# The projection into u in seven quarter products, and one explicit list of steps, in a block attention with a gated MLP

## The chip, the cores and the metric

The kernel runs on one core of one Trainium2 chip. The metric is the time of one execution on the device in microseconds (us), the median of several runs. A profiled execution gives the trace; its span is counted from the first to the last instruction. The engines are PE (TensorE, matmuls; PEld is its weight load), DVE (VectorE), ACT (ScalarE), POOL (GpSimd) and SP (SyncE, which issues the transfers here). SPq is the queue of SP.

## The reference

Attention within chunks of 64 tokens, for 8 batches, 8 heads, 576 tokens and head size 64; its output x, as a matrix of 576 x 512 for each batch, goes through a gated MLP.

```python
scores = scale * np.matmul(q_c, k_c.transpose(0, 1, 2, 4, 3))     # chunks of 64
attn = softmax(scores)                                            # over the chunk
x = np.matmul(attn, v_c)                                          # per batch 576 x 512
h = gelu_tanh(x @ w_in)                                           # w_in 512 x 1024
u, v = h[..., :512], h[..., 512:]
v_n = (v - mean(v)) / np.sqrt(var(v) + 1e-06) * g_ln
v_s = np.einsum('ts,bsd->btd', w_sg, v_n) + b_sg[None, :, None]   # w_sg 576 x 576
out = x + (u * v_s) @ w_out                                       # w_out 512 x 512
```

## The kernel before

The 36 attention tiles of 128 tokens (four and a half make a batch of 576 tokens) and the MLP of 8 batches run as one stream. A matrix product in full accuracy is made of three matmuls on fp32r operands: every operand is held as a high part and a low part (`xh`, `xl` for x; `gh`, `gl` for the gated product; `win_h`, `win_l` for w_in), and low x high, high x low and high x high are added up in PSUM.

The steps of a tile t: `att_load` (SP loads q, k and v), `att_scores` (S for one tile, P for a pair; matmuls into the two `banks` of PSUM, then the softmax on DVE, ACT and POOL), `att_transpose` (T; from tile 5 on the 32x32 blocks are transposed on DVE, copied by ACT, and four quarters of 32 partitions are swapped: `ptT<-blocks`, two copies on ACT, two on DVE by `SWAP_ON_ACT`) and `att_out` (O, or Q for a pair; matmuls into a `pm` buffer of PSUM, then the split into `xh`, `xl` and the plain `xf` in `keep`).

The steps of a batch b: `v_unit` (v0 to v3, and in each even batch v4 for the odd rows of two batches: 12 matmuls of 512 columns, gelu on ACT, statistics on DVE, the power -1/2 on POOL in line 545, then scaling and splitting), `u_unit` (u0 to u3: 24 matmuls of 128x288, line 573, and a gelu into the tile `u2`), `s_unit` (s0 to s3: the product of w_sg with v, 28 matmuls, then the multiplication with u on DVE) and the product with w_out. That last one is written in seven products of quarters for batches from `QUARTERS_FROM` = 2 on (Strassen's scheme in Winograd's form): `o_product` p1, p5, p2, p6, p3, p7, p4, each 12 matmuls of 128x288 in line 660. Sums of w_out's quarters are made once by POOL (`sum_step`) and kept in the DRAM tensor `factors`; `load_factor` brings each product's factor back into a ring of four places. Batches 0 and 1 use `o_unit` with whole w_out.

`pm` has three buffers in PSUM. The tile `u2` has one buffer: it holds u of a batch, then the gated product and its sums, then three of four quarters of the output until the stores to `out_dram` have read them.

w_in and w_out come as float64; `pair_begin` and `pair_end`, and `double_begin` and `double_end`, make high and low parts from their words on ACT, DVE and PE (lines 136 to 189). `START` lists the steps of the weights and of batches 0 and 1 (W and w: a quarter of w_in's v half; X and x: of its u half; Y: an eighth of w_out; B, C and K: the factors). From batch 2 on, the last loop of the function writes v's, u's, s's and p's in a fixed order and puts the attention of later tiles behind units by `SLOTS`. A step writes all its instructions at once. The framework's scheduler then orders the instructions of each engine by its own costs; only the matmuls of batches from 2 on (`pin`) and a few others keep the program's order. Each engine works through its own order strictly.

Of the kernel before, what the change touches and what calls it, by code (L numbers as in the profile page):

```python
# [17 lines left out]
ALU = mybir.AluOpType  # L18
# [27 lines left out]
START = """  # L46
L0 A0 S0 D8 L1 L2 A1 L3 S1 W0 w0 W1 w1 A4 S2 T0 O0 T1 O1 W2 T2 w2 X0 M0 W3 w3 S3 O2
S4 T3 O3 v00 x0 X1 X2 T4 v01 v02 O4 x1 x2 X3 v03 G0 A8 u00 g0 P5 g1 x3 g2 g3 u01 v04 g4 T5
u02 T6 u03 s00 P7 Q5 s01 s02 T7 T8 s03 v10 Y0 Q7 Y1 v11 Y2 u10 u11 Y3 v12 Y4 v13 u12 Y5 Y6 Y7 A10
u13 o00 P9 s10 T9 T10 s11 s12 A12 A14 s13 P11 Q9 o01 B0 o02 B1 B2 T11 B3 o03 T12 A15 o10 B4 C5 o11 B5  # L50
B6 S13 T13 Q11 o12 B7 C6 o13 B8 B9 A17 v20 v21 C7 O13 K0 P14 v22
"""

PE_TILES = 5

SWAP_ON_ACT = (1,)
# [4 lines left out]

SLOTS = {
    1: "v1:T0 v1:T1 u0:S23 u0:T2 u0:O01 s0:T3 s0:S4 s0:O23 s3:T4 p6:S56",
    0: "v0:O4 u0:T5 u2:S78 s0:T6 s1:O56 s2:T8 p5:T7 p3:S9A p3:O78",
}

QUARTERS_FROM = 2
PRODUCTS = (1, 5, 2, 6, 3, 7, 4)  # L70
RING = 4
# [4 lines left out]
SINGLE_ON_ACT = False  # L76
# [14 lines left out]
def block_attention_gated_mlp(ctx: ExitStack, tc: tile.TileContext, qkv, w_in, w_out, w_sg, g_ln, b_sg, out):  # L91
# [10 lines left out]
    def split(hi, lo, src, hi_eng, lo_eng):  # L102
        if hi_eng is nc.scalar:
            nc.scalar.copy(hi, src)  # L104
        else:
            hi_eng.tensor_copy(hi, src)
        lo_eng.tensor_tensor(lo, src, hi.bitcast(F32), op=ALU.subtract)  # L107


# [22 lines left out]

    def pick(step):
        return nc.gpsimd if step in ON_POOL else nc.vector

    def high_word(f, hw):

        nc.scalar.activation(f.bitcast(F32), hw.bitcast(F32), AF.Abs, scale=2.0**16)  # L140
        nc.vector.tensor_scalar(f.bitcast(F32), f.bitcast(F32), ZERO64, TOP64, op0=ALU.max, op1=ALU.min)
        nc.vector.tensor_scalar(f, f, 4, 1, op0=ALU.logical_shift_left, op1=ALU.logical_shift_right)
        nc.vector.scalar_tensor_tensor(f, hw, -0x80000000, f, op0=ALU.bitwise_and, op1=ALU.bitwise_or)

    def double_begin(n, st, eng):

        raw, fi, ri = st[:, : 2 * n], st[:, 2 * n : 3 * n], st[:, 3 * n : 4 * n]
# [15 lines left out]

    def pair_begin(n, st):
# [6 lines left out]
        high_word(f, pair[:, :, 1])  # L171
# [3 lines left out]
        q, lw, top = words[:, :n], words[:, 1::4], p.bitcast(U16)[:, 1::2]  # L175
        nc.vector.scalar_tensor_tensor(q, lw, 9, top, op0=ALU.logical_shift_right, op1=ALU.bitwise_or)

    def pair_end(n, hi, lo, st):
# [3 lines left out]
        ps = ps_m.tile([P, 2, 512], F32, name="pm")[:, 0, :n]  # L182
        shape = lambda a: a.rearrange("p (k c) -> p k c", k=hi.shape[1]) if len(hi.shape) == 3 else a
        nc.scalar.mul(hi, shape(f), -1.0)
        terms = [(ident, f), (low[0], q), (low[1], p), (ident_r, hi)]
        for i, (a, c) in enumerate(terms):
            out_ps = shape(ps) if c is hi else ps
            nc.tensor.matmul(out_ps, a, c, start=(i == 0), stop=(i == len(terms) - 1))  # L188
        nc.scalar.mul(lo, shape(ps), -1.0)
# [28 lines left out]
    def u_w_begin(dt):  # L218
        pair_begin(DH, staged["u", dt])

    def u_w_end(dt):
        cols = slice(dt * P, (dt + 1) * P)
        pair_end(DH, win_h[:, :, cols], win_l[:, :, cols], staged["u", dt])

    def o_w(et, half):
# [8 lines left out]
        double_begin(n, st, pick("Z"))  # L234
        double_end(n, wout_h[:, rows, cols], wout_l[:, rows, cols], st, pick("Y"))


    factors = nc.dram_tensor("factors", (7, P, 2, 2, 2 * P), F32).ap()
    ring, loads, sums = [], [0], []
# [4 lines left out]
    def load_factor():  # L244
        n = loads[0]
        loads[0] += 1
        if n < 7 * (B - QUARTERS_FROM):
            nc.sync.dma_start(out=factor_place(n).bitcast(F32), in_=factors[n % 7])

    def quarters():  # L250
        return [
            a[:, 2 * c : 2 * c + 2, 2 * r * P : 2 * (r + 1) * P] for r in range(2) for c in range(2) for a in (wout_h, wout_l)
        ]

    def sum_step(n):
# [12 lines left out]
        tc.keep_in_program_order(nc.gpsimd.tensor_tensor(o, a, c, op=op))  # L268

    def keep_factor(p, parts):  # L270
        for a, part in enumerate(parts):
            tc.keep_in_program_order(nc.sync.dma_start(out=factors[PRODUCTS.index(p), :, a], in_=part.bitcast(F32)))

    def split_sum(p):

        hi, lo = (
            tmp.tile([P, S], F32R, name="fac", tag="tmp")[:, : 4 * P].rearrange("p (k e) -> p k e", k=2) for _ in range(2)
        )
        src = sums[(5, 6, 7, 3).index(p)]
        tc.keep_in_program_order(nc.scalar.copy(hi, src))  # L280
        nc.vector.tensor_tensor(lo, src, hi.bitcast(F32), op=ALU.subtract)
        keep_factor(p, (hi, lo))
        if p == 3:
            for i in range(2):
                r = const.tile([P, KT * DM], F32R, name=f"ring_{i}", tag=f"wout_{i}")
                ring.append(r.rearrange("p (n a k e) -> p n a k e", n=2, a=2, k=2))
            for _ in range(RING):
                load_factor()

    def keep_quarters(_):  # L290
        parts = quarters()
        for p, i in ((1, 0), (2, 2), (4, 6)):
            keep_factor(p, parts[i : i + 2])
# [14 lines left out]
    def split_w_sg(i):  # L308
        nonlocal wsg_h, wsg_l
        st, odd, bt = staged["s"]  # L310
        if i == 0:
            wsg_h, wsg_l = (w_sg_tile(i).rearrange("p (i s) -> p i s", i=5) for i in range(2))
            nc.gpsimd.memset(wsg_l[64:128, 4, :].bitcast(F32), 0.0)
        hi, lo = wsg_h[:, i, :], wsg_l[:, i, :]
        if i < 4:
            split(hi, lo, st[:, i, :], nc.scalar, nc.vector)
            return
        nc.scalar.copy(hi, odd)
        nc.vector.tensor_tensor(lo[0:ODD], odd[0:ODD], hi[0:ODD].bitcast(F32), op=ALU.subtract)
# [60 lines left out]
    pinned = [False]  # L380

    def pin(ins):
        if pinned[0]:
            tc.keep_in_program_order(ins)

    def att_scores(*tiles):

        if tiles[0] < PE_TILES:
            for t in tiles:
# [6 lines left out]
                softmax((t,), sc)  # L396
            return
        for i, t in enumerate(tiles):
            qt = state[t]
            sc = banks[:, :, i * HP * D : (i + 1) * HP * D].rearrange("p c (hp s) -> p c hp s", hp=HP)  # L400
            for h in range(H):
                for c in range(2):
                    r, o = slice(c * D, (c + 1) * D), half(t, h, c)
                    pin(nc.tensor.matmul(sc[o, c, h // 2, :], qt[r, 0, h, :], qt[r, 1, h, :], start=True, stop=True))  # L404
# [428 lines left out]
```

## Time and profile before

| | us |
|---|---|
| median of 3 runs | 500.79 (500.75 to 500.91) |
| the profiled execution | 500.32 |
| its span | 498.5 |
| mean granted PE clock in it | 1.00 |

The page gives for each engine the time in which it was busy, as a share of the span; matmuls overlap, so a busy PE isn't PE at its peak rate. The chain that ended last is followed back from the last instruction, at each step to what released it. A row of a group has the line, engine, operation, output and inputs with their shapes and count, then the busy time, the mean of one in ns, and the idle time ahead of it with what ended it. The rows that the prediction rests on are shown there.

### The profile page before, as it was taken

How to read it: one execution, taken by the hardware profiler on the slowest of the kernel's cores; microseconds unless marked ns; L12 is line 12 of the kernel's file. 1: busy time of each engine (PE TensorE's matmuls, PEld its weight loads, DVE VectorE, ACT ScalarE, POOL GpSimd, SP SyncE). 2: the span in 40 equal slices, each digit the busy share in tenths (PEclk: the TensorE clock that was granted, in tenths of full speed). 3: DMA queues.
4: the chain of work that ended last, by engine and by line, in shares of the span. 5: the costliest groups of instructions: out<-in, count | busy, mean ns of one | idle time of the engine just before them, and what ended most of it. 6: DMA issues, size and time to landing. Idle time of an engine off the chain costs nothing.

```text
span 498.5 us, 12331 instructions
## 1 busy us (share of the span) xinstructions
PE 485.9 (97%) x5167; PEld 449.6 (90%) x5172; DVE 378.1 (76%) x697; ACT 281.5 (56%) x489; POOL 89.1 (18%) x82
## 2 busy tenths in 40 slices
PE   5989999999999999999999999999999999999996
PEld 4667899899999899989999899988999899998996
DVE  7898769987789875988589675998679675876065
ACT  5798777753445775566752574557752564543130
POOL 0113000121084222022210312022120322002000
PEclk9999999999999999999999999999999999999999
DMA  8858001256146971694348600695447700181006
GB/s 330 304 170 241 6 3 43 87 152 169 56 145 220 275 257 52 208 264 169 87 126 258 197 1 11 202 283 162 120 128 228 226 1 1 48 291 55 0 10 212
DMA packets 61355, 72.27 MB, mean 145 GB/s; under 512 B 36082, under 2 KB 47858, under 8 KB 61300
## 3 DMA queue, kind: packets, MB, share of 16 engines
q1 hardware_dynamic: 61300, 71.49, 46.6%
q8 instruction: 40, 0.66, 0.5%
q14 instruction: 15, 0.12, 0.1%
HBM read 58.36 MB, written 13.11 MB: 143 GB/s over the span
## 4 chain that ended last, share of the span: by engine, by line
PE 88%; DVE 7%; ACT 2%; DMA 2%; SPq 0%; issue 0%; POOL 0%; ACTq 0%
PE pm L593 22%; PE pm L573 21%; PE pm L536 19%; PE pm L660 14%; PE pm L713 5%; PE banks L404 3%; PE pm L492 3%; DMA qkv_t<-qkv 2%; PE pm L188 1%; ACT pt L425 1%; DVE pt L433 1%; DVE nmax L417 1%; DVE gl L107 1%; DVE gt L602 1%; DVE xl L107 0%; PE banks L473 0%
## 5 line engine op out<-in xcount | busy, mean ns | idle before, releaser
L593 PE MATMUL pm<-wsg,v 128*128 128x288 f32 x768 | 108.1, 296 | 0.0
L593 PEld LDWEIGHTS pm<-wsg,v 128*128 128x128 f32 x768 | 103.8, 189 | 0.5
L545 POOL TENSOR_TENSOR sm<-sm,neg_half 128x1 f32<-128x1 f32 x36 | 36.9, 1024 | 152.0 <-DVE sm L544 139.8
L433 POOL TENSOR_TENSOR pt<-pt,den 128x1024 f32<-128x1024 f32 (+1 forms) x15 | 26.0, 1733 | 171.2 <-DVE den L431 157.3
L573 PE MATMUL pm<-xl,win_h 128*128 128x288 f32 x256 | 55.3, 297 | 1.0 <-DVE xl L107 1.0
L573 PE MATMUL pm<-xh,win_l 128*128 128x288 f32 x256 | 55.5, 298 | 0.0
L573 PE MATMUL pm<-xh,win_h 128*128 128x288 f32 x256 | 55.0, 296 | 0.0
L536 PE MATMUL pm<-win_h,xl 128*128 128x512 f32 x128 | 51.2, 400 | 0.2 <-ACT pt L425 0.2
L536 PE MATMUL pm<-win_h,xh 128*128 128x512 f32 x128 | 50.7, 396 | 0.0
L536 PE MATMUL pm<-win_l,xh 128*128 128x512 f32 x128 | 50.6, 395 | 0.0
L553 ACT ACTIVATE v<-hs,sm 128x512 fp32r<-128x512 f32 x32 | 23.2, 724 | 43.4 <-POOL sm L545 43.3
L104 ACT CAST gh<-u 128x576 fp32r<-128x576 f32 x24 | 16.2, 675 | 48.5 <-POOL u L617 29.7
L573 PEld LDWEIGHTS pm<-xh,win_l 128*128 128x128 f32 x256 | 41.5, 188 | 1.3
L573 PEld LDWEIGHTS pm<-xl,win_h 128*128 128x128 f32 x256 | 41.1, 188 | 1.3 <-DVE xl L107 1.3
L573 PEld LDWEIGHTS pm<-xh,win_h 128*128 128x128 f32 x256 | 41.0, 188 | 0.0
L660 PE MATMUL pm<-gh,ring 128*128 128x288 f32 x192 | 40.3, 296 | 0.0
L554 DVE SCALAR_TENSOR_TENSOR v<-hs,sm,v 128x512 fp32r<-128x512 f32 x32 | 24.0, 750 | 18.5 <-ACT v L553 18.3
L598 DVE TENSOR_TENSOR u<-pm,u 128x576 f32<-128x576 f32 x24 | 18.1, 753 | 20.4 <-PE pm L593 20.3
L660 PE MATMUL pm<-tv,ring 128*128 128x288 f32 x216 | 32.2, 297 | 0.0
L542 DVE BATCH_NORM_STATS2 sm<-hs 128x6 f32<-128x512 f32 x36 | 24.5, 683 | 9.9 <-ACT hs L539 9.8
L660 PEld LDWEIGHTS pm<-gh,ring 128*128 128x128 f32 x192 | 31.4, 188 | 0.1
L428 ACT ACTIVATE pt<-pt 128x1024 f32<-128x1024 f32 (+1 forms) x19 | 18.0, 949 | 22.2 <-DVE pt L427 21.9
(146 smaller groups left out, 1018.8 us busy)
## 6 DMA issues: line engine op xcount, KB each, us to landing
ring<-factors SPq DMA_DIRECT2D x42, 512.0 KB, 4.6
qkv_t<-qkv SPq DMA_DIRECT2D x32, 512.0 KB, 4.7
qkv_t<-qkv SPq DMA_DIRECT2D x124, 64.0 KB, 3.9
out_dram<-u SPq DMA_DIRECT2D x18, 288.0 KB, 5.2
out_dram<-ot SPq DMA_DIRECT2D x14, 288.0 KB, 2.7
qkv_t<-qkv SPq DMA_DIRECT2D x3, 768.0 KB, 7.6
wsg<-w_in SPq DMA_DIRECT2D x4, 512.0 KB, 5.3
wout<-w_in SPq DMA_DIRECT2D x4, 512.0 KB, 7.0
```

Of the source, the lines that this page charges most:

```text
L428: nc.scalar.activation(pt, pt, AF.Exp, scale=scale)
L433: eng.tensor_tensor(pt, pt, den.unsqueeze(2).broadcast_to([P, n, D]), op=ALU.mult)
L536: pin(nc.tensor.matmul(pv, a[:, kt, tok], c[:, kt, DH:], start=(i == 0), stop=(i == 11)))
L542: nc.vector.bn_stats(st, h)
L545: nc.gpsimd.tensor_tensor(rs, rs, neg_half, op=ALU.pow)
L553: nc.scalar.mul(hi, h, rs)
L554: nc.vector.scalar_tensor_tensor(lo, h, rs, hi.bitcast(F32), op0=ALU.mult, op1=ALU.subtract)
L573: pin(nc.tensor.matmul(pm[:, j, :HS], a[:, kt, dc], c[:, kt, j * HS : (j + 1) * HS], start=(i == 0), stop=(i == 11)))
L593: pin(nc.tensor.matmul(pm[:, j, :HS], a[:, dc], c[:, m, j * HS : (j + 1) * HS], start=(i == 0), stop=(i == len(ops) - 1)))
L598: nc.vector.tensor_tensor(g, pm[:, :, :HS], g, op=ALU.mult)
L660: pin(nc.tensor.matmul(pm[:, e, :HS], a[:, k, e * P : (e + 1) * P], c[:, k, :], start=starts and i == 0, stop=i == len(ops) - 1, skip_grou ...
L713: nc.tensor.matmul(pm[:, j, :HS], a[:, kt, ec], c[:, kt, j * HS : (j + 1) * HS], start=(i == 0), stop=(i == len(ops) - 1),)
```

## The change

1. From batch 2 on the projection into u is made of seven products of quarters as well. `u_product` (q1, q5, q2, q6, q3, q7, q4) has 12 matmuls each and collects in three `pm` buffers; x and z of them are added up as in `o_product`, and the gelu follows each finished quarter. Three results are copied out of PSUM by ACT, three are added by DVE.
2. The right factors of q5, q7, q6 and q4 are sums of x's quarters. `x_quarters` (z25, z27, z26, z24 for batch 2) makes them: a sum on POOL into the quarter (1, 0) of `u2`, a cast on ACT into the high part, a subtraction on DVE for the low part, in the tile `xt`, which takes over the place of w_in's u half.
3. The left factors are sums of w_in's quarters, made once: `sum_product` (E0 to E3) adds high and low parts by matmuls with the identity and with its negative, and ACT and DVE split the result. They go to `factors`, which has 14 rows now, and the ring loads 84 factors in place of 42.
4. w_in's two halves are tiles of their own (`wv_h`, `wv_l`; `wu_h`, `wu_l`).
5. `SWAP_ON_ACT` is (0, 1): all four swaps of a tile's transposition are on ACT. `SINGLE_ON_ACT` is True: the softmax of the single tiles 13, 22 and 31 is made by eight exponentials on ACT with their sums.
6. Every step is a generator that stops (`yield`) before each instruction that another engine must have prepared. `ORDER` lists the whole program as some 2,400 entries; each entry runs one step on to its next stop. `tc.manual_schedule()` keeps every engine's instructions in that order. The loads of the ring (`f`) and of tiles (`A`) are entries too.

```diff
+SWAP_ON_ACT = (0, 1)
+ORDER = """
+L0 L1 A0 M0 L2 L3 A1 W0 A2 A3 W0 A4 W1 W0 W0 W1 w0 W0 W1 S0 W0 W1 w0 w1 S0 W2 W1 S0 W1 S0
...
+v30 p27 p23 f16 P18 p27 P18 P18 p24 v30 v30 Q16 v30 f17 p24 v30 T19 p24 v31 Q16 v31 A20 T18 T19 Q16 v30 T19 T19 v30
...
-SINGLE_ON_ACT = False
+SINGLE_ON_ACT = True
...
+    ctx.enter_context(tc.manual_schedule())
...
+    wu = wu_tile("wu").rearrange("p (a k c) -> p a k c", a=2, k=KT)
+    wu_h, wu_l = wu[:, 0], wu[:, 1]
...
-    factors = nc.dram_tensor("factors", (7, P, 2, 2, 2 * P), F32).ap()
+    factors = nc.dram_tensor("factors", (14, P, 2, 2, 2 * P), F32).ap()
+    order = [i for b in range(O_QUARTERS_FROM, B) for i in ([*range(7)] if b >= U_QUARTERS_FROM else []) + [*range(7, 14)]]
...
+    def sum_product(n):
...
+        pos, neg = (((h21, l21, h22, l22), ()), ((), (h11, l11)), ((), (h12, l12)), ((h11, l11), (h21, l21)))[n]
+        terms = [(ident_r, a) for a in pos] + [(held["neg"], a) for a in neg]
+        for i, (a, c) in enumerate(terms):
+            nc.tensor.matmul(
+                ps, a, c, start=n in (0, 3) and i == 0, stop=i == len(terms) - 1, skip_group_check=n in (1, 2)
+            )
+        yield
+        hi, lo = factor_tiles()
+        nc.scalar.mul(hi, ps, -1.0 if n == 2 else 1.0)
...
+    def x_quarters(b, p):
...
+        begin_u(b)
+        t = quarter_of(u2[b], 1, 0)
+        a, c = {5: (x(0, 1), x(0, 0)), 7: (x(1, 1), x(0, 1)), 6: (t, x(0, 0)), 4: (x(1, 0), t)}[p]
+        X_SUM[p].tensor_tensor(t, a, c, op=ALU.add if p == 6 else ALU.subtract)
+        hi, lo = x_right[p]
+        yield
+        nc.scalar.copy(hi, t)
+        yield
+        X_LOW[p].tensor_tensor(lo, t, hi.bitcast(F32), op=ALU.subtract)
+
+    def u_product(b, p):
+        at = {1: "x", 5: "y", 2: "z", 6: "x", 3: "y", 7: "x", 4: "x"}[p]
+        starts = p in (1, 5, 2)
...
+        ops = [(a, c, k) for k in range(2) for a, c in ((wl, hi), (wh, lo), (wh, hi))]
+        for e in range(2):
+            for i, (a, c, k) in enumerate(ops):
+                nc.tensor.matmul(
+                    pm[:, e, :HS], a[:, k, e * P : (e + 1) * P], c[:, k, :],
+                    start=starts and i == 0, stop=i == len(ops) - 1, skip_group_check=not starts,
+                )
+        yield
...
+        if p in (1, 5, 6):
+            nc.scalar.copy(o, src) if p in U_KEPT_ON_ACT else nc.vector.tensor_copy(o, src)
+            return
+        if p != 4:
+            nc.vector.tensor_tensor(o, src, o, op=ALU.add)
+            yield
+        nc.scalar.activation(o, src if p == 4 else o, AF.Gelu_apprx_tanh, scale=-1.0)
...
+    begun = {}
+    for step in ORDER.split():
+        if step not in begun:
+            begun[step] = iter(steps[step[0]](int(step[1:])) or ())
+        next(begun[step], None)
```

POOL's order in the part of batch 3 in which its v's and u's are made (`sm` is the statistics of a v, `pt` a softmax, the number behind u is that of the tile `u2` of a batch). Before:

```order
30 L433 TENSOR_TENSOR pt<-pt,den 128x1024
31 L545 TENSOR_TENSOR sm<-sm,neg_half 128x1 x4
32 L433 TENSOR_TENSOR pt<-pt,den 128x1024
33 L617 TENSOR_TENSOR u_3016<-u_3016 128x288
34 L433 TENSOR_TENSOR pt<-pt,den 128x512
```

and now:

```order
34 L667 TENSOR_TENSOR sm<-sm,neg_half 128x1
35 L763 TENSOR_TENSOR u_3011<-xf 128x2x288
36 L667 TENSOR_TENSOR sm<-sm,neg_half 128x1
37 L763 TENSOR_TENSOR u_3011<-xf 128x2x288
38 L667 TENSOR_TENSOR sm<-sm,neg_half 128x1
39 L763 TENSOR_TENSOR u_3011<-u_3011,xf 128x2x288
40 L667 TENSOR_TENSOR sm<-sm,neg_half 128x1
41 L763 TENSOR_TENSOR u_3011<-xf,u_3011 128x2x288
42 L539 TENSOR_TENSOR pt<-pt,den 128x1024
```

The four sums of x's quarters (L763) stand between the powers of the four v's, and the first of them is the first to write batch 3's `u2`.

SP's order at the end of batch 2: the ring's loads, the stores of the output's quarters (p2 from `ot`, the other three from `u2`) and the loads of the next attention tiles. Before:

```order
72 L671 DMA out_dram<-u_2337 128x2x288
73 L372 DMA qkv_t<-qkv 128x1024
74 L377 DMA qkv_t<-qkv 64x4x64 x4
75 L372 DMA qkv_t<-qkv 128x1024
76 L377 DMA qkv_t<-qkv 64x4x64 x4
77 L248 DMA ring_2306<-factors 128x1024
78 L671 DMA out_dram<-u_2337 128x2x288
79 L248 DMA ring_2307<-factors 128x1024
80 L671 DMA out_dram<-u_2337 128x2x288
```

and now:

```order
75 L860 DMA out_dram<-ot 128x2x288
76 L311 DMA ring_2171<-factors 128x1024 x2
77 L860 DMA out_dram<-u_2245 128x2x288
78 L311 DMA ring_2170<-factors 128x1024
79 L860 DMA out_dram<-u_2245 128x2x288
80 L311 DMA ring_2170<-factors 128x1024
81 L860 DMA out_dram<-u_2245 128x2x288
82 L476 DMA qkv_t<-qkv 128x1024
83 L481 DMA qkv_t<-qkv 64x4x64 x4
```

The last two stores stood behind the loads of two attention tiles; now all stand ahead of them.

ACT's order in the start, up to the cast of tile 1's x (`xh<-xf`, its second), which the first v waits for (`wsg_`, `wout_` are the places in which w_in's quarters are staged). Before:

```order
19 L189 ACTIVATE win_l<-pm 128x512
20 L104 CAST xh<-xf 128x2x4x64
21 L445 COPY ptT<-banks 128x512
22 L522 CAST xodd_285<-xh 128x4x64
23 L522 CAST xodd_286<-xl 128x4x64
24 L140 ACTIVATE wsg_201<-wsg_201 128x512
25 L184 ACTIVATE win_h<-wout_159 128x512
26 L512 COPY xf<-banks 128x2x4x64
27 L189 ACTIVATE win_l<-pm 128x512
28 L104 CAST xh<-xf 128x2x4x64
```

and now:

```order
20 L186 ACTIVATE wsg_188<-wsg_188 128x512
21 L526 ACTIVATE pt,den<-pm,nmax 128x64 x8
22 L552 COPY ptT<-banks 128x512
23 L531 ACTIVATE pt<-pt 128x512
24 L186 ACTIVATE wsg_215<-wsg_215 128x512
25 L186 ACTIVATE wout_256<-wout_256 128x512
26 L248 ACTIVATE wv_l<-pm 128x512
27 L552 COPY ptT<-banks 128x512
28 L240 ACTIVATE wu<-wsg_188 128x4x128
29 L622 COPY xf<-banks 128x2x4x64
30 L640 CAST xodd_324<-xh 128x4x64
31 L624 CAST xh<-xf 128x2x4x64
```

Passes for the first three quarters of w_in's u half (188, 215, 256) have moved ahead of that cast, and 188 ahead of tile 2's exponentials (row 21).

More of the change, by code (lines that the diff above doesn't have):

```diff
@@ L40 @@
 QKV_BUFS = 4
[L46 to L51, printed above, removed]
-"""
-PE_TILES = 5
-SWAP_ON_ACT = (1,)
@@ L267, in sum_step, with keep_factor @@
         )[n]
[L268 to L270 removed]
+        nc.gpsimd.tensor_tensor(o, a, c, op=op)
+    def keep_factor(of, p, parts):
+        row = PRODUCTS.index(p) + (7 if of == "o" else 0)
         for a, part in enumerate(parts):
[L272 removed]
+            nc.sync.dma_start(out=factors[row, :, a], in_=part.bitcast(F32))
@@ L281, in split_sum @@
         nc.vector.tensor_tensor(lo, src, hi.bitcast(F32), op=ALU.subtract)
[L282 to L291, printed above, removed]
+        yield
+        keep_factor("o", p, (hi, lo))
@@ L292, in keep_quarters, with begin_ring @@
+    def begin_ring():
+        for i in range(2):
+            r = const.tile([P, KT * DM], F32R, name=f"ring_{i}", tag=f"wout_{i}")
+            ring.append(r.rearrange("p (n a k e) -> p n a k e", n=2, a=2, k=2))
+        for _ in range(RING):
+            load_factor()
+    def keep_quarters(of):
+        parts = quarters(of)
         for p, i in ((1, 0), (2, 2), (4, 6)):
-            keep_factor(p, parts[i : i + 2])
+            keep_factor(of, p, parts[i : i + 2])
     def load_w_sg():
@@ L403, in att_scores @@
                     r, o = slice(c * D, (c + 1) * D), half(t, h, c)
-                    pin(nc.tensor.matmul(sc[o, c, h // 2, :], qt[r, 0, h, :], qt[r, 1, h, :], start=True, stop=True))
-        softmax(tiles, banks[:, :, : len(tiles) * HP * D].rearrange("p c (k s) -> p c k s", s=D))
+                    nc.tensor.matmul(sc[o, c, h // 2, :], qt[r, 0, h, :], qt[r, 1, h, :], start=True, stop=True)
+        yield from softmax(tiles, banks[:, :, : len(tiles) * HP * D].rearrange("p c (k s) -> p c k s", s=D))
     def softmax(tiles, sc):
@@ L564, in block_attention_gated_mlp, with begin_u @@
     u2 = {}
+    def begin_u(b):
+        if b not in u2:
+            u2[b] = mp.tile([P, KT, S], F32, name="u2", tag="u2")
     def u_unit(b, dt):
@@ L684, in o_product @@
             add(ot, held[1])
-            store(0, 0, ot)
+            yield from store(0, 0, ot)
         elif p == 6:
@@ L690, in o_product @@
             add(o, o)
-            store(0, 1, o)
+            yield from store(0, 1, o)
         elif p == 7:
@@ L700, in o_product @@
             add(o, o if last else x(1, 0))
-            store(1, 0, o)
+            yield from store(1, 0, o)
     def o_unit(b, et):
```

444 lines of the change are left out of this document (276 added, 168 removed).

## The prediction

> **What bounds the kernel now.** I read the head of the page first, then the chain that ended last in order of time, then the waits of TensorE.
>
> ```profile
> span 498.5 us, 12331 instructions
> PE 485.9 (97%) x5167; PEld 449.6 (90%) x5172; DVE 378.1 (76%) x697; ACT 281.5 (56%) x489; POOL 89.1 (18%) x82
> PE 88%; DVE 7%; ACT 2%; DMA 2%; SPq 0%; issue 0%; POOL 0%; ACTq 0%
> ...
> PE pm L395 <- DMA qkv_t<-qkv: 6.1, 2, 5.8
> PE pm L573 <- DVE xl L107: 1.0, 1, 1.0
> ```
>
> TensorE (PE) is busy for 97% of the span and the chain runs through it for 88%. Its only waits are the first load and one microsecond on DVE. Busy time alone proves little, because matmuls overlap, so the chain in order of time has to show at what rate the work goes by.
>
> ```profile
> 49.56 3.20 PE pm L573 x24
> ...
> 92.25 1.14 DVE xl L107
> 93.44 6.27 PE pm L573 x45
> ...
> 218.31 1.59 PE pm L660 x12
> 219.90 8.40 PE pm L536 x36
> 228.29 3.20 PE pm L573 x24
> 231.49 1.09 PE banks L404 x64
> 232.58 0.96 PE pm L492 x63
> ...
> 492.67 1.85 PE pm L660 x12
> 494.54 0.76 DVE u L666
> ```
>
> A unit of u (L573) is 24 matmuls in 3.20 us, 133 ns each; a unit of v (L536) is 12 in 2.80 us (8.40 for 36), 233 ns each; a product (L660) is 12 in 1.59. These rates hold from 93.44 to 494.5 without a hole. There a matmul less is time less, as long as every other engine keeps up. Before 93 us the work waits for weights, loads and DVE: the first v matmul starts only at 29.33.
>
> ```profile
> 29.33 0.50 PE L536 MATMUL pm<-win_h,xl 128*128 128x512 f32 x1
> ```
>
> **The change, part by part.** *Matmuls.* In each of batches 2 to 7, 96 matmuls for u become seven products of 12, so 84. That removes 6 x 12 = 72 at 133 ns: **-9.6 us**. The sums of w_in's quarters add 12 matmuls of 512 columns, at 233 ns **+2.8 us**; the nearest row of such matmuls is dearer:
>
> ```profile
> L188 PE MATMUL pm<-win_h,ident 128*128 128x512 f32 x8 | 4.7, 582 | 0.8 <-ACT win_h L184 0.8
> ```
>
> At 0.582 it were 7.0, but a mean of overlapping single matmuls in a start full of waits says little of a run in a dense stream, so I keep 2.8 and hold 7.0 as the upper end.
>
> *The other engines.* The new passes have these relatives:
>
> ```profile
> L598 DVE TENSOR_TENSOR u<-pm,u 128x576 f32<-128x576 f32 x24 | 18.1, 753 | 20.4 <-PE pm L593 20.3
> L107 DVE TENSOR_TENSOR tv<-u,tv 128x576 fp32r<-128x576 f32 x18 | 13.4, 742 | 0.0
> L104 ACT CAST tv<-u 128x576 fp32r<-128x576 f32 x18 | 11.5, 672 | 13.2 <-DVE u L679 13.2
> L580 ACT ACTIVATE u<-pm 128x576 f32<-128x576 f32 x32 | 20.6, 648 | 8.2 <-PE pm L573 7.0 <-DVE fac L281 0.8
> L268 POOL TENSOR_TENSOR sums<-wout 128x512 f32<-128x512 f32 x4 | 5.2, 1332 | 0.0
> L617 POOL TENSOR_TENSOR u<-u 128x288 f32<-128x288 f32 x12 | 9.6, 802 | 37.8 <-DVE u L598 37.8
> L459 DVE COPY ptT<-blocks 32x256 f32<-32x256 f32 x62 | 22.7, 365 | 10.3 <-ACT ptT L452 8.8
> L457 ACT COPY ptT<-blocks 32x256 f32<-32x256 f32 x62 | 25.0, 404 | 1.3
> ```
>
> Per batch DVE gets three sums out of PSUM (0.753) and four low parts (0.742), 5.2 us, in six batches 31 us; it loses the 62 half swaps, 22.7 us. DVE ends near 387 us, still under four fifths. ACT gets those swaps at 0.404 (25 us), 24 casts at 0.672 (16 us), 18 copies out of PSUM at the 0.648 of u's gelu (12 us) and the softmax of three single tiles, so it rises from 281 to some 340 us, 70%. POOL gets 24 sums of 128x576: on the line through 802 ns for 288 columns and 1332 for 512 that is 1.48 us each, 36 us, so 125. None of the three becomes the bound by its sum, so all this is hidden, provided PE is not kept waiting on a latency. If it were not hidden, one batch's additions on DVE alone would cost 5.2 us.
>
> *The latency that is new.* All seven results and POOL's sums go to the one u buffer. In before that buffer is first written by the gelu of u0, after five v's or four and a u. Now POOL's first sum of a batch writes it, so that sum waits for the store of the last quarter of the batch ahead (p4). Three sums, each followed by ACT's cast and DVE's low part, have to pass one after the other through the same quarter before product 6. The rows of the store:
>
> ```profile
> 224.88 0.39 SPq L671 DMA_DIRECT2D out_dram<-u  x1
> ...
> ring<-factors SPq DMA_DIRECT2D x42, 512.0 KB, 4.6
> ...
> out_dram<-u SPq DMA_DIRECT2D x18, 288.0 KB, 5.2
> out_dram<-ot SPq DMA_DIRECT2D x14, 288.0 KB, 2.7
> ```
>
> The product p4 of batch 2 ended at 219.90 (its row above), and the store was only issued at 224.88, behind loads on SP. In the new SP order it stands ahead of the next tiles' loads, so I take 0.4 for the issue. From the end of p4: sum 0.75, issue 0.4, landing 5.2, three links of 1.48 + 0.67 + 0.74: 15.1 us with no queueing at all. PE, by the new order, needs product 6 after one output step (L492), three v's, three products and one score step (L404) in batch 3: 1.0 + 3 x 2.8 + 3 x 1.59 + 1.09 = 15.3 us later; in batches 4 to 7, counted in the same way, after 17.1, 16.3, 17.1 and 16.0. If each of the nine passes queues for 0.3 us (about half of one pass on an engine that is 70 to 80% busy), the chain is 17.8 and PE waits 2.5, 0.7, 1.5, 0.7 and 1.8: 7.2 us. If the store lands in 2.7 as the ot stores do, nothing waits. I take **+2.5 us**, nearer to none, because the v work in between is what these engines do anyway; the ends are 0 and, with POOL at the 1.905 us of its rows of 1024 columns, 1.3 more in each batch, 13.7:
>
> ```profile
> L433 POOL TENSOR_TENSOR pt<-pt,den 128x1024 f32<-128x1024 f32 x12 | 22.9, 1905 | 158.6 <-DVE den L431 144.6 <-DMA qkv_t<-qkv 13.9
> ```
>
> Factor loads double, 42 more of 512 KB, on queues that are at 46.6% of their time. A load is issued when the product four places earlier has ended, at least three products or 4.8 us ahead, against 4.6 us to land; before, seven products in a row ran on this margin without a wait of PE. I cost it at nothing; cover gone, each late load costs some tenths, for 84 loads up to 8 us.
>
> *The start.* The list also reorders the first 90 us. On ACT, four passes of 0.6 to 0.67 us more, less one of 0.4, stand ahead of the cast for the first v, some 2.2 us, and one of these waits for a weight load that is now issued behind all the first tiles:
>
> ```profile
> 0.00:25.00 25.00, 18.75 (x245) 14.02 (x249) 20.14 (x45) 16.04 (x54) 1.96 (x7) 1.00 0.88 317
> wsg<-w_in SPq DMA_DIRECT2D x4, 512.0 KB, 5.3
> ```
>
> Four weight halves of 512 KB, the row of g and five tiles of 768 KB go ahead of it, 6.3 million bytes, at the 317 GB/s of this window 20 us after the first issue, so it lands near 22 to 23, and v00 starts up to 3.7 us later than 29.33. On the other side DVE reaches the last low part of tile 4, on which the first u waits, with some 5 us less work ahead of it, and the low part of tiles 7 and 8 (the 92.25 row) with 3 us less. Between 29.33 and 49.56 PE now has some 15.3 us of work (four v's 11.2, twelve weight matmuls 2.8, the small ones of tiles 2 to 4) in 20.2, so at most 4.9 can be won there and 1.0 at 93. Between +3.7 and -5.9 I take **-1.5 us**.
>
> *The end.* One more addition (0.75) stands between the last two; PE's last 1.85 us cover part of it: **+0.4 us**.
>
> *Sum.* The profiled execution took 500.32 us, 498.5 of it the span. 500.32 - 9.6 + 2.8 + 2.5 - 1.5 + 0.4 = 494.9. The median of the runs, 500.79, is 0.5 above the profiled one, so **495.4 us**.
>
> **A rule against the trace.** POOL's two-input work slows DVE at times:
>
> ```profile
> 140.69 2.54 POOL L268 TENSOR_TENSOR sums<-wout 128x512 f32<-128x512 f32 x2
> ...
> 142.24 2.51 DVE L459 COPY ptT<-blocks 32x256 f32<-32x256 f32 x2 [0.76 <-ACT ptT L452]
> ...
> 27.79 1.27 POOL L107 TENSOR_TENSOR xl<-xf,xh 128x512 fp32r<-128x512 f32 x1 [3.31 <-ACT xh L104]
> ...
> 28.66 0.95 DVE L176 SCALAR_TENSOR_TENSOR wsg<-wsg 128x512 uint16<-128x512 uint16 x1
> ...
> 228.58 0.58 DVE L459 COPY ptT<-blocks 32x256 f32<-32x256 f32 x2
> ...
> L176 DVE SCALAR_TENSOR_TENSOR wout<-wout 128x512 uint16<-128x512 uint16 x4 | 2.7, 684 | 0.0
> ```
>
> Two swaps took 2.51 us beside POOL's sums, and 0.58 with POOL idle; a two-input pass took 0.95 beside POOL, against 0.684 in its like rows. The swaps now leave DVE, but the low parts read two SBUF tensors while POOL does the sums. The Trainium skill, "SBUF — State Buffer", section "Who interferes with whom", says that a DVE instruction with two SBUF inputs contends with a GpSimd instruction that reads SBUF, and that the passes in a two-port mode are locked out entirely; by it the chain of sums is slower than its separate rows. The trace agrees for the swaps, 2.51 against 0.58.
>
> **The rivals.**
> 1. *The chain through the one u buffer decides* (slower). For it: the store left SP 5 us after its product in before. Against it: the new SP order puts it first, and the list places other work there. At the upper price, 13.7, the time is 494.9 - 2.5 + 13.7 + 0.5 = 506.6. It turns the change slower from 1.6 us a batch, because without stalls the gain is 7.9 us over five batches.
> 2. *POOL and DVE hold each other up.* At 0.27 us (0.95 - 0.68) for each of three links in five batches, 4.0 us: 499.4.
> 3. *The start gains all it can and nothing waits*: -5.9 instead of -1.5 and 0 instead of 2.5, 488.5.
> 4. *The list loses at the start what the matmuls win*: +3.7 in place of -1.5, 500.6. For it speaks the load that is now issued late; against it that ACT had 9 us free in the first 25.
>
> **How the numbers follow.** Forecast 0.52 (492 to 498), rival 1 0.17, rival 2 0.13, rival 3 0.13, rival 4 0.05. The range 489 to 503 leaves out the upper half of rival 1 and some of rival 3; the dearer end of the new w_in sums, 4.2 more, and late factor loads lie within it. Measurement tells about 0.2%, 1.0 us, from no change. Faster: the forecast, rival 3 and some two thirds of rival 2, 0.73; within 0.2%: rival 4 and parts of rivals 1 and 2, 0.10; slower 0.17.
>
> **What would show it.** The matmul step is right if the u products of one batch take 84 x 133 ns; PE should then be as dense as before, with granted clock 1.0. The chain shows as waits of PE on xt or of POOL's first sum on a store of out_dram, once per batch from batch 3. The start shows in the time of the first v matmul (29.33 before, up to 33) and of the first u (49.56 before). I am wrong if PE waits for factor loads, or if several microseconds of waits stand in batches where none of these steps are.

## The result and the profile after

| | before | changed |
|---|---|---|
| median of 6 runs, us | 500.85 (500.52 to 501.40) | 504.48 (502.73 to 504.94) |
| ratio | | 1.0065 (95%: 1.0050 to 1.0081) |
| the profiled execution, us | 500.32 | 504.94 |
| its span, us | 498.5 | 503.2 |

The change makes the kernel slower by 0.65%. The page of the changed kernel, its head and the shares of the chain by engine:

```profile
span 503.2 us, 12519 instructions
PE 483.1 (96%) x5112; PEld 441.1 (88%) x5112; DVE 390.4 (78%) x678; ACT 342.9 (68%) x645; POOL 120.6 (24%) x106
PE 76%; DVE 8%; ACT 7%; DMA 6%; POOL 2%; issue 1%; SPq 0%; POOLq 0%; DVEq 0%; ACTq 0%
```

PE has less to do, as forecast, but the chain runs through it for 76% instead of 88%: DVE, ACT and the transfers are on it with 21%. The waits of PE (engine, line, what it waited for: us in total, times, the longest; those of the start and one of 0.2 us left out; before there was one of 1.0 us behind the start):

```profile
PE pm L781 <- ACT xf L633: 1.2, 1, 1.2
PE pm L654 <- DVE xl L631: 1.1, 1, 1.1
...
PE pm L654 <- ACT hs L658: 0.9, 2, 0.4
PE pm L781 <- ACT u L790: 0.7, 1, 0.7
...
PE pm L654 <- ACT xf L633: 0.6, 1, 0.6
PE pm L781 <- ACT xt L766: 0.6, 1, 0.6
PE pm L781 <- DVE xt L768: 0.4, 1, 0.4
PE pm L849 <- DMA ring<-factors: 0.2, 1, 0.2
```

Only two rows are on `xt`, the new chain. The others stand at v units (L654), at products that need a `pm` buffer (L781 on the copies L633 and L790), and one at a load of the ring.

The waits don't hold all of the lost time: they count from a matmul's modelled end, and the start behind a wait is followed late as well (the matmul at 227.09 by the next after 0.33 us, against 0.23 in a dense run). So I also count PE's **standing**: from the starts of the recorded matmuls, the time that is not covered by the dense spacing of each (133 ns for 288 columns, 233 for 512, 17 for the 64x64 ones, 111 for 128x128).

| standing of PE, us | to 100 us | 100 to 210 (batch 2) | 210 to the last matmul | behind it |
|---|---|---|---|---|
| before | 23.8 | 0.8 | 2.8 | 4.2 |
| changed | 22.3 | 3.0 | 11.7 | 4.8 |

Before, five records of the start are missing (PE x5167, PEld x5172), 1.2 us, so its 23.8 is nearer to 22.6. The start won 0.3 us, the end lost 0.6, and the stretch between has 14.7 in place of 3.6.

Where the standing comes from is read in the chain in order of time. A seam between two batches (start us, us, what):

```profile
217.49 2.81 PE pm L654 x12
...
220.36 1.28 ACT L658
...
221.66 0.61 ACT hs L658
...
222.29 0.71 DVE sm L662
...
223.39 0.66 DVE u L854
224.05 0.62 DVE blocks L556
224.67 0.63 DVE hs L669
225.30 0.62 DVE blocks L556
225.92 1.12 DVE xl L631
...
227.09 0.96 PE pm L654 x3
```

The first v of batch 3 ends; only then ACT loads its table (1.28), then comes the gelu, and DVE's statistics wait for that. Behind the statistics, in DVE's fixed order, stand the addition of p4 (L854), two transposes of later tiles and the low part of x (L631) for which PE waits until 227.09; it stood for 1.4 us. The gelu's load is on this path although ACT was free for 1.20 us before it.

The new chain, in batch 7:

```profile
447.89 1.22 DVE xl L631
449.11 0.68 DVE u L854
449.80 5.78 DMA out_dram<-u
...
455.80 1.69 POOL u L763
...
457.51 0.68 ACT xt L766
...
458.22 0.76 DVE xt L768
...
463.42 1.45 DVE v L677
...
465.15 0.68 DVE xt L768
...
465.87 3.33 PE pm L781 x23
```

Its parts are those of the prediction (store 5.8, sum 1.7, cast 0.7, low part 0.8), and its last low part ends at 465.83, just ahead of the product. Between them stand v's statistics and v's low parts in DVE's order, one low part with 1.45 us (L677); rival 2 below comes back to it.

### The profile page after: what moved, and what is told of

Same layout as the page of the kernel before. It is cut to its first block, busy times and chain, and to the rows that moved or that the text cites. A ratio compares the mean times of both kernels' runs of the same rounds, so it can differ in the third digit from the quotient of the medians.

```text
span 503.2 us, 12519 instructions
## 1 busy us (share of the span) xinstructions
PE 483.1 (96%) x5112; PEld 441.1 (88%) x5112; DVE 390.4 (78%) x678; ACT 342.9 (68%) x645; POOL 120.6 (24%) x106
## 4 chain that ended last, share of the span: by engine, by line
PE 76%; DVE 8%; ACT 7%; DMA 6%; POOL 2%; issue 1%; SPq 0%; POOLq 0%; DVEq 0%; ACTq 0%
PE pm L731 22%; PE pm L654 14%; PE pm L849 11%; PE pm L781 10%; PE pm L703 5%; PE pm L907 4%; PE pm L601 3%; PE banks L502 3%; DMA out_dram<-u 2%; PE pm L246 2%; DMA qkv_t<-qkv 2%; ACT L658 1%; ACT ptT L566 1%; POOL u L763 1%; DMA ring<-factors 1%
## 5 line engine op out<-in xcount | busy, mean ns | idle before, releaser
L667 POOL TENSOR_TENSOR sm<-sm,neg_half 128x1 f32<-128x1 f32 x36 | 28.5, 794 | 109.0 <-DVE sm L665 107.6
L654 PE MATMUL pm<-wv_h,xl 128*128 128x512 f32 x128 | 51.7, 404 | 2.7 <-DVE xl L631 1.1
L566 ACT COPY ptT<-blocks 32x256 f32<-32x256 f32 x124 | 50.1, 404 | 2.2
L654 PE MATMUL pm<-wv_h,xh 128*128 128x512 f32 x128 | 50.6, 395 | 0.0
L654 PE MATMUL pm<-wv_l,xh 128*128 128x512 f32 x128 | 50.6, 395 | 0.0
L781 PE MATMUL pm<-xt,ring 128*128 128x288 f32 x288 | 44.0, 300 | 1.2 <-ACT xt L766 0.6
L781 PEld LDWEIGHTS pm<-xt,ring 128*128 128x128 f32 x288 | 39.5, 188 | 3.0 <-DVE xt L768 1.3
L781 PE MATMUL pm<-xh,ring 128*128 128x288 f32 x144 | 31.9, 297 | 1.9 <-ACT xf L633 1.2
L654 PEld LDWEIGHTS pm<-wv_h,xl 128*128 128x128 f32 x128 | 24.0, 188 | 9.3 <-DVE xl L631 1.6
L677 DVE SCALAR_TENSOR_TENSOR v<-hs,sm,v 128x512 fp32r<-128x512 f32 x32 | 28.1, 881 | 5.0 <-ACT v L675 4.8
L849 PEld LDWEIGHTS pm<-tv,ring 128*128 128x128 f32 x216 | 29.7, 188 | 1.1 <-issue 0.6
L654 PEld LDWEIGHTS pm<-wv_h,xh 128*128 128x128 f32 x128 | 24.0, 188 | 5.8
L654 PEld LDWEIGHTS pm<-wv_l,xh 128*128 128x128 f32 x128 | 24.1, 188 | 4.8
```

The lines of the kernel that those rows point to most:

```text
L566: nc.scalar.copy(ptT[q[1 - a], :, a, :], blocks[q[a], :, 1 - a, :])
L654: nc.tensor.matmul(pv, a[:, kt, tok], c[:, kt, :], start=(i == 0), stop=(i == 11))
L667: nc.gpsimd.tensor_tensor(rs, rs, neg_half, op=ALU.pow)
L677: nc.vector.scalar_tensor_tensor(lo, h, rs, hi.bitcast(F32), op0=ALU.mult, op1=ALU.subtract)
L781: nc.tensor.matmul(pm[:, e, :HS], a[:, k, e * P : (e + 1) * P], c[:, k, :], start=starts and i == 0, stop=i == len(ops) - 1, skip_group_ch ...
L849: nc.tensor.matmul(pm[:, e, :HS], a[:, k, e * P : (e + 1) * P], c[:, k, :], start=starts and i == 0, stop=i == len(ops) - 1, skip_group_ch ...
```

## The experiments

Theory C: the standing comes from the chain of x's sums through the one `u2` buffer. Theory A: ACT and DVE have too much to do in the stage of v and q, and any wait that is taken away comes back at another place. Theories B, D and F (order of the list at the seams, table load, ring loads) were formed on the way. Unless said otherwise each kernel is the changed one with the edit shown. Behind each time stand its ratio to the kernel before, which took 500.7 to 500.9 beside it, and the 95% interval of the ratio; 0.001 of it is 0.5 us. Two kernels that weren't run beside each other are better compared by these ratios than by their times.

### Eight kernels that tell the parts apart

**The list without the quarter products.** The steps z, E, N, k, q6, q7 and q4 and the loads f of u's factors are taken out of `ORDER`; q1, q5, q2, q3 become u0 to u3 (in batch 5, u0 after the third part of Q25).

```diff
-U_QUARTERS_FROM = 2
+U_QUARTERS_FROM = 8
```

> The list without the quarter products of u: batches 2 to 7 make u by whole units again (4 of 24 matmuls, put where q1, q5, q2 and q3 began), w_in's sums, x's sums and half of the factor loads are gone, all else of the list and both constants stay. PE has 6.8 us more work than the changed kernel (72 matmuls of 133 ns, less 12 of 233). If the new passes of ACT, DVE and POOL cause the stalls that PE has after 100 us (14.7 us in the changed kernel's trace against 3.5 before), they fall to about 4 here and the time is 500 to 501, as before the change. If the list stalls by itself, whatever stands in it, the time is 508 to 511.

518.58 us (ratio 1.0365, 1.0332 to 1.0398). The wait of PE that is longest after the start's:

```profile
PE pm L583 <- ACT ptT L548: 7.1, 5, 2.4
```

The output steps of the attention wait for swaps on ACT, five times. Units of 24 matmuls don't fit the places of products of 12, so this run doesn't tell what a list made for units would do; the new passes aren't needed for a list to stall.

**A place of its own for x's sums.** `held["t"]` is the seventh slot of `xt`, `tf` the same as plain fp32.

```diff
-        begin_u(b)
-        t = quarter_of(u2[b], 1, 0)
+        t = held["t"]
+        tf = t.bitcast(F32)
```

> The sums of x's quarters go to a place of their own in the rest of xt instead of the quarter (1,0) of u2, so that they no longer wait for the last store of the batch ahead; they are written rounded to fp32r there, so their low parts are nil (an other result in u, the same instructions). Theory C (the chain through the one u2 buffer): the waits of PE on xt and the one on the copy L790 go, 3 to 4 us with the restarts, 500.5 to 501.5. Theory A (ACT and DVE are late with passes of every kind): these waits are replaced by waits on other passes of the same engines, 503.5 to 504.5.

505.46 (1.0092, 1.0077 to 1.0107), no gain; but the standing moved: from 210 us on it is 9.5 instead of 11.7, and in batch 2 6.3 instead of 3.0. The place is part of w_in's u half, whose last readers are w_in's sums of that time; the wait for them is what I take for the cause in batch 2. So the chain seems worth some 2 us, and this edit gave them back in batch 2. The same edit from batch 3 on:

```diff
+        if b < 3:
+            begin_u(b)
+        t = held["t"] if b >= 3 else quarter_of(u2[b], 1, 0)
```

> As e2, but batch 2 keeps its sums in u2 (in e2 they had to wait there for the last readers of w_in's u half); the sums of batches 3 to 7 are in a place of their own, rounded to fp32r. Theory C, as far as e2 bears it out (from batch 3 on 2.25 us less standing of PE): 501.8 to 502.8. If the chain costs nothing: 504 to 505.

501.76 (1.0022, 1.0009 to 1.0035): 2.7 us less. From 210 us on PE stands 9.3. Theory C is right about its price and wrong as the whole cause.

**Work moved between ACT and DVE.** Two edits, each by itself:

```diff
-SWAP_ON_ACT = (0, 1)
+SWAP_ON_ACT = (1,)
```

> SWAP_ON_ACT is (1,) again: 62 half swaps (25 us of ACT) go back to DVE (23 us there). Theory A with ACT as the late engine: the waits of PE on ACT's gelu and on copies and casts of x fall by half or more, 499 to 502. Theory A with DVE as the late engine: worse than 504.5 by some us. Theory C: the chain has two passes on ACT for every one on DVE, 504 to 505.

```diff
-U_KEPT_ON_ACT = (1, 5, 6)
+U_KEPT_ON_ACT = ()
```

> The copies of q1, q5 and q6 out of PSUM are made by DVE instead of ACT (18 passes, 12 us off ACT, some 13 us more on DVE, to 403). Theory A with ACT late: 501 to 503.5. Theory A with DVE late: 505 to 508. Theory C: no change beyond 1 us, 504 to 505.

509.82 (1.0184, 1.0168 to 1.0199) and 509.92 (1.0183, 1.0167 to 1.0200). The busy times of the two:

```profile
PE 484.2 (95%) x5112; PEld 441.5 (87%) x5112; DVE 416.6 (82%) x740; ACT 318.5 (63%) x583; POOL 120.9 (24%) x106
```

```profile
PE 484.7 (95%) x5112; PEld 441.5 (87%) x5112; DVE 401.6 (79%) x696; ACT 333.4 (66%) x627; POOL 119.4 (23%) x106
```

26 us more on DVE cost 5.3, and 11 us cost 5.4: the price goes by the place of a pass, not by its length. The second kind stands in the stage of v and q, and the longest waits of PE behind the start in that kernel are on DVE's low parts of x's sums (3.4 us in four). Theory A with ACT as the late engine falls: more work costs on DVE. The busy times by stretch of the changed kernel (start:end, us, then busy time and count of PE, PEld, DVE, ACT, POOL, then the granted clock, the share of the DMA engines and GB/s):

```profile
303.00:331.00 28.00, 28.00 (x322) 27.54 (x321) 24.07 (x35) 18.09 (x28) 3.53 (x3) 1.00 0.58 173
335.00:359.00 24.00, 22.08 (x302) 18.83 (x304) 18.62 (x32) 20.44 (x34) 10.16 (x9) 1.00 0.87 261
```

The first is a stage of s and p: PE is full with DVE at 86%. The second is a stage of v and q: PE falls to 92% although DVE has 78% and ACT 85%. I read it as passes that wait for each other in turn, not as a sum of work that stops PE; e11 and e12 below bear that out, where 25 us of passes taken away win 1.1.

**The seams rewritten.** In batches 3 and 5 the attention's output comes ahead of the first v and of p4 (batch 3 before and after, number behind the point: part of the step); in batches 4 and 6 the copy that frees the `pm` buffer of the attention's output comes ahead of the gelu.

```text
-v30.1 p27.2 p23.3 f16.1 P18.5 p27.3 P18.6 P18.7 p24.1 v30.2 v30.3 Q16.1
+Q16.1 p27.2 p23.3 f16.1 P18.5 p27.3 P18.6 P18.7 Q16.2 p24.1 v30.1 Q16.3 Q16.4 p24.2 v30.2 v30.3
```

> The changed kernel with four places of the list rewritten, where the first v of batches 3 to 6 begins: in batches 3 and 5 the attention's last output step (Q16, Q25) comes ahead of the first v and of p4, and its high and low parts ahead of that v's gelu and statistics on ACT and DVE; in batches 4 and 6 the copy that frees the pm buffer of O22 and O31 comes ahead of the gelu. PE stood 1.49, 0.59, 0.94 and 0.59 us there in the changed kernel's trace. Theory B (the list brings x's parts and pm buffers too late at these seams): 500.5 to 502. Theory A (DVE and ACT simply have too much to do, and any place only moves the wait): 503.5 to 505.

508.18 (1.0147, 1.0128 to 1.0165). At 225 us PE no longer stands, but 2.05 us at the first product of q 6 us later (it waits for a gelu of v, 1.7), and at the other three places it stands longer than before. Theory B falls in this form: an attention output that comes earlier on ACT and DVE delays the gelus behind it.

> e5 and e6 together. Theories B and C together, 3.6 and 2.25 us from 504.5: 498 to 499.5, below the kernel before. Theory A: 503 to 505.

507.68 (1.0133, 1.0117 to 1.0149), with both edits: as e5.

**No list.** Only the line of the manual schedule is left out.

```diff
-    ctx.enter_context(tc.manual_schedule())
```

> The changed kernel without the manual schedule: the same entries in program order, but the framework's scheduler orders each engine's instructions by its own costs, as before the change. If the list's order is what costs (theory B), the time is 498 to 503; if the scheduler does worse with these passes, PE stands more and the time is 506 to 515.

554.52 (1.1072, 1.1050 to 1.1093). With the new passes the framework's scheduler does 50 us worse than the list; the list isn't a free choice beside the products.

### The table load, the low parts, the loads

**An early table load.** A gelu of one column, step H, ahead of the first v's gelu in `ORDER`.

```diff
+        "H": lambda k: nc.scalar.activation(spare, neg_half, AF.Gelu_apprx_tanh) and None,
```

> The changed kernel with a gelu of one column (128x1, of a constant) ahead of the first v's gelu of batches 3 to 7 on ACT: it waits for nothing, so that the table load of 1.28 us no longer stands behind the wait for the first v's product. Theory D (at the seams PE waits for a pm buffer and for x's low part behind this table load): the stalls of 1.49, 0.59, 0.94 and 0.59 us shrink by up to 1.28 each, 501.0 to 502.3. Theory A (ACT and DVE have too much to do in this stage, so that a wait removed comes back later): 503.5 to 505.

504.30 (1.0073, 1.0045 to 1.0102): four runs, two at 503.0 and two at 505.6. The profiled one is of the latter, and its longest wait after the start's is new:

```profile
PE pm L769 <- DMA ring<-factors: 2.2, 1, 2.2
```

At the four seams it stands 0.54 us and three times below 0.15, as theory D says; in batch 2 it stands 3.72 us at 182. The stall costs more than its wait: from 186.35 to 189.76 us, right behind it, this trace has a granted clock of 0.50, and 14 matmuls of 288 columns start 0.24 us apart in place of 0.13. The gain and this stall hide each other, so this run alone can't be read. With the own place:

> e9 and e6 together (501.76 was e6). Theory D: 498.3 to 500.0, below the kernel before. Theory A: 501 to 502.

499.71 (0.9972, 0.9955 to 0.9990), 2.1 below e6 (2.5 by the ratios). The step H is worth that beside the own place.

**Passes taken off the chain.** In the kernel of e6 the low parts are left out from batch 3 on; then the casts too.

```diff
         yield
+        if b >= 3:
+            return
         X_LOW[p].tensor_tensor(lo, tf, hi.bitcast(F32), op=ALU.subtract)
```

> e6 with the low parts of x's quarter sums left out from batch 3 on (DVE loses 20 passes of 0.75, 15 us; ACT and POOL lose nothing; the low place keeps what batch 2 left there). Theory A with DVE as the engine that is short in the v and q stage: PE's standing after 100 us (11.3 us in e6, 3.5 before the change) falls by half of the difference, 497 to 499. If DVE isn't short: 501 to 502.

```diff
+            h7, h6 = (x_right[i][0].bitcast(F32) for i in (7, 6))
+            a, c = {5: (x(0, 1), x(0, 0)), 7: (x(1, 1), x(0, 1)), 6: (h7, x(0, 0)), 4: (x(1, 0), h6)}[p]
+            X_SUM[p].tensor_tensor(hi, a, c, op=ALU.add if p == 6 else ALU.subtract)
+            return
```

> e11, and POOL writes each sum straight into its high place from batch 3 on, so that ACT loses 20 casts of 0.67 (13 us) as well. Theory A with ACT as the engine that is short: 1.5 to 4 us below e11. With DVE alone short: as e11 within 1 us.

500.64 and 500.49 (both 1.0001, 0.999 to 1.001): 1.1 us less for 14 us of DVE's busy time, and nothing more for 11 us of ACT's. Theory A as a lack of capacity is worth about 1 us, on DVE.

**The late loads of batch 2.** What SP issued at 178 us in the changed kernel, and how long the ring load at 179.5 took to land (min, median, max of the one load), there and then in e9 and e10:

```profile
174.18 4.09 SPq L481 DMA_DIRECT2D qkv_t<-qkv  x4
178.38 1.03 SPq L339 DMA_DIRECT2D factors<-fac  x2
179.50 5.53 SPq L311 DMA_DIRECT2D ring<-factors  x4
```

```profile
DMA to landing us min/median/max: 5.8/5.8/5.8
```

```profile
DMA to landing us min/median/max: 6.7/6.7/6.7
```

```profile
DMA to landing us min/median/max: 3.5/3.5/3.5
```

It carries q3's factor. Landed at 185.3 in the changed kernel, it fits the start of q3 at 185.41; the table of waits blames the copy L790, which ended at the same time. PE stood 1.07, 3.72 and below 0.15 us there. The four loads ahead of it are v of tile 17, needed much later; they are moved:

```diff
             nc.sync.dma_start(out=qt[:, 0:2], in_=qkv[t, :, 0:2])
+            if t == 17:
+                state[t] = qt
+                yield
...
-f6 q22
+f6 A17 q22
```

> The changed kernel with one load moved on SP: the four loads of tile 17's v, which Q16 needs only 40 us later, go behind the ring loads f4 to f6 of batch 2 (q and k of that tile stay). Theory F (the first ring loads of batch 2 are late, since they stand behind these loads and share the queues with them: PE stood 1.07 us there in the changed kernel's trace, 3.72 in e9's): the stall at 182 us falls below 0.5 in the trace and the median goes to 502.5 to 503.7. If the load is late for another reason: 504 to 505, with 1 to 4 us at 182.

504.11 (1.0066, 1.0051 to 1.0080). In the trace nothing is left of the stall at 182, and batch 2 stands 1.9 in place of 3.0; the median gains only 0.4, less than theory F gave, and by the ratios (1.0065 without the edit) nothing: the stall in the trace is explained, a gain in time isn't shown. With the other two edits:

> e10 with the loads of tile 17 moved as in e13. e10's runs went from 497.3 to 501.7 with a median of 499.71. Theory F: fewer runs near 501, a median of 498.5 to 499.4. If not: 499.5 to 500.

498.72 (0.9960, 0.9946 to 0.9974), below the kernel before. It is 1.0 below e10 too, but the intervals of the two overlap. Two more runs complete the four corners (all with tile 17's loads moved):

> e13 with the early table load (sums again through u2): with e13 (504.11), e14 (498.72) and e17 four corners of the two edits. If the two are independent: 504.1 less 2.1, 501.5 to 502.5. If what PE wins at the seams it waits again at the chain, which starts at the store of p4 and not at PE: 503.3 to 504.3, with more standing at the first product that reads xt (1.77 us in batch 7 in e13's trace).

> e13 with the place of its own from batch 3 on, without the early table load. e6 was 501.76. If the loads of tile 17 are worth what e10 against e14 shows (1.0): 500.7 to 501.3. If nothing: 501.5 to 502.

| | sums through u2 | own place from batch 3 |
|---|---|---|
| table load behind the wait | e13 504.11 | e17 501.27 |
| early table load | e16 502.13 | e14 498.72 |

e16 has 1.0042 (1.0022 to 1.0063), e17 1.0009 (0.9997 to 1.0020). By the medians the early load is worth 2.0 and 2.6, the own place 2.8 and 3.4. The columns pair kernels that were not run beside each other, and so do the rows; by the ratios it is 1.2 and 2.5, and 2.9 and 4.1. So each size is known to about 1 us, and the 1.2 of the early load beside sums through u2, where the intervals overlap, isn't clear of noise. Within that, neither gain takes the other away. ACT's rows of time at the seam in e16:

```profile
217.39 1.28 ACT L928 ACT_TABLE_LOAD   x1
218.69 0.20 ACT L928 ACTIVATE spare<-neg_half 128x1 f32<-128x1 f32 x1
218.79 0.58 ACT L649 ACTIVATE hs<-pm 128x512 f32<-128x512 f32 x1
```

The load now starts while PE still makes the v. That v's last matmul starts at 217.72 here, so the gelu starts 1.1 us behind it; in the changed kernel it was 1.8 (219.89 and 221.66).

**Low parts on POOL** (in the kernel of e10):

```diff
-X_LOW_ON = {5: "vector", 6: "vector", 7: "vector", 4: "vector"}
+X_LOW_ON = {5: "gpsimd", 6: "gpsimd", 7: "gpsimd", 4: "gpsimd"}
```

> e10 with the low parts of x's quarter sums on POOL in place of DVE (DVE loses 24 passes, 18 us; POOL gets 24 of some 1.4 us, 34 us, ahead of v's powers in its queue). If DVE's load in the v and q stage is what is left of the stalls (theory A): 498 to 499.3, like the step from e6 to e11. If v's powers come late behind POOL's passes: 500.5 to 504.

512.49 (1.0241, 1.0218 to 1.0264). PE waits for the chain itself:

```profile
PE pm L772 <- POOL xt L759: 6.4, 5, 1.9
```

A low part takes 1.52 us on POOL instead of 0.75 on DVE, and the edit costs 12.8 us (e10 to e15). The longer links aren't its only effect: DVE lost 24 passes of 0.75, 18 us, but its busy time fell only from 390.8 to 387.0, since other passes grew, those over v above all (the one that takes v's mean off and multiplies by `g_bc` went from 756 to 912 ns in the mean). So the run tells that POOL is the wrong place for this work, and not what DVE's load is worth.

## Why the prediction was wrong

*The matmuls: right.* Four products of q and one third of w_in's sums in the chain in order of time:

```profile
172.06 0.91 PE pm L370 x4
...
410.01 6.56 PE pm L781 x48
```

137 ns a matmul where the next one waits for nothing (133 forecast), and 0.91 for four sums, so 2.7 us for twelve, near the 2.8 taken and not the 7.0 of the upper end. -9.6 and +2.8 stand.

*The loads of the engines: right as sums, wrong as an argument.* DVE 390, ACT 343, POOL 121 against 387, 340 and 125. Luck is in it for POOL: its 36 powers took 28.5 us in place of 36.9, and its other work more than forecast. From "none of the three becomes the bound by its sum" I went to "all this is hidden, provided PE is not kept waiting on a latency", and then priced one latency only, the chain. That is **the step that failed**: the places where PE meets the other engines were not walked through. At the seams the old order had none of these waits; the new list puts an attention output behind the first v and p4, where three `pm` buffers, a table load and DVE's queue meet. The sums of the profiled execution (the first line is worked out from the counts, the others are counted):

| | forecast | measured |
|---|---|---|
| matmuls, 72 less and 12 more (by the spacing) | -6.8 | -6.8 |
| start | -1.5 | -0.3 |
| standing after 100 us | +2.5 | +11.1 |
| end | +0.4 | +0.6 |
| in all | -5.4 | +4.6 |

*Of the 11.1*, the chain is worth 2 to 4 (e6, e17, e14), about the 2.5 that were forecast, though that was a choice between 0 and 13.7 (in batch 7 it took 16.7 us from the addition of p4 at 449.11 to the last low part; the forecast had 15.1 without queueing, which is 15.0 by its own terms, and 17.8 with it); the table load at the seams 1 to 2.6 (e10, e16, e14); the loads of tile 17 ahead of the ring's 0 to 1.0 (e13, e14), which isn't clear of noise; the low parts on DVE 1.1 (e11). The first three edits together took off 5.8 us (e14; 5.3 by the ratios), so with the low parts, if these add up, it is 6 to 7. The rest, 4 to 5, isn't settled: the largest place is 1.3 us in batch 5, where a product waits for a `pm` buffer that a copy of x frees (L633). That wait was not tried by itself, and e5 and e15 show that single moves can cost more than they win.

*Rival 1* had the right sign and the wrong price: at 2 to 4 us its chain alone would not have made the kernel slower. *Rival 2* is seen, but at another pass than the prediction looked at. The low parts (751 ns, 742 for their relatives before) were never beside a sum of POOL, since each waits for the cast of that sum. The pass that makes the low part of a v (L554, now L677), which reads two tensors in SBUF as well, was. Before and after:

```profile
L554 DVE SCALAR_TENSOR_TENSOR v<-hs,sm,v 128x512 fp32r<-128x512 f32 x32 | 24.0, 750 | 18.5 <-ACT v L553 18.3
```

```profile
L677 DVE SCALAR_TENSOR_TENSOR v<-hs,sm,v 128x512 fp32r<-128x512 f32 x32 | 28.1, 881 | 5.0 <-ACT v L675 4.8
...
L768 DVE TENSOR_TENSOR xt<-u,xt 128x576 fp32r<-128x576 f32 x24 | 18.0, 751 | 5.0 <-ACT xt L766 4.9
...
L763 POOL TENSOR_TENSOR u<-xf 128x576 f32<-128x576 f32 x12 | 19.0, 1586 | 24.5 <-DVE xt L768 8.4 <-ACT xf L633 7.6 <-ACT ptT L566 5.0
```

```profile
231.50 1.43 POOL L763 TENSOR_TENSOR u<-xf 128x576 f32<-128x576 f32 x1 [0.73 <-DVE xt L768]
231.94 1.54 DVE L677 SCALAR_TENSOR_TENSOR v<-hs,sm,v 128x512 fp32r<-128x512 f32 x1
```

Nine of these 32 passes took 0.80 to 1.54 us, all of them beside a sum of POOL; the others took 0.75 at most. POOL's sums took 1.42 to 1.88 us, against 1.48 estimated. That is 4.1 us more on DVE in the stage where PE stands; one such pass is on the chain of batch 7 above (463.42). What it costs the kernel was not tried, since no run has the quarter products without POOL's sums; it may be a part of the 4 to 5 us. The Trainium skill, "SBUF — State Buffer", section "Who interferes with whom", has a DVE instruction with two inputs in SBUF contend with a GpSimd instruction that reads SBUF. The trace agrees at this pass: 1.54 us beside a sum, 0.75 without one.

*The factor loads* I costed at nothing, with 4.8 us of margin against 4.6 to land. The same load landed in 3.5, 5.8 and 6.7 in three traces: a median of landings is no cover for a margin of the same size. This can also spread the runs: of e9's four, the two at 505.6 have a mean granted clock of 0.996 and 0.997, as the stall in the trace of one of them shows it, and the two at 503.0 have 0.999.

*The start*: the first v came at 33.11 (forecast: up to 33) and the first u at 47.51, 2.05 earlier; the wait at 93 is gone. By the standing it won 0.3, not 1.5.

The change can be mended, as far as the runs go: e14 takes 498.72, 0.4% below the kernel before (0.9946 to 0.9974), with sums of x's quarters that are rounded to fp32r from batch 3 on.

## What to carry to other kernels

Where a matmul-bound kernel gets fewer matmuls for more passes on other engines, their busy share says little: walk from seam to seam and write down, for each place at which the matmul engine needs a buffer or an operand, which queue it comes out of and what stands ahead of it there. Fewer matmuls also shorten every margin that was counted in matmuls, those of loads and of chains of small passes. A fixed order for all engines holds only for the work that it was made for: moving 11 us from one engine to another cost 5 us here (e4), and taking 14 us of other passes away altogether won 1 (e11).

## What was not expected of the hardware

A table load on ACT stands behind the wait of the activation that needs it, even where ACT is idle:

```profile
220.36 1.28 ACT L658 ACT_TABLE_LOAD   x1 [1.20 <-PE pm L654]
221.66 0.60 ACT L658 ACTIVATE hs<-pm 128x512 f32<-128x512 f32 x1
```

ACT was idle for 1.20 us ahead of it. A one-column gelu of 0.20 us that waits for nothing brings the load forward; over the four seams that have such a load it is worth 1 to 2.6 us. The Trainium skill, "ScalarE: Activation LUTs", section "What ACT_TABLE_LOAD costs", gives 1283 ns for the load, which the trace shows as well (1.28), and some 1380 ns of draining on top; here the gelu follows 0.02 us behind the load, and in e16 the load follows 0.02 us behind the activation ahead of it (it starts at 217.39), so no such time is seen.
